# Token lists of a mixture of experts: scattered through DRAM slots instead of built by one-hot matmuls

## The chip, the cores and the metric

One core of a Trainium2 chip runs the kernel. The metric is the device time in microseconds (us). Engines: TensorE (PE, with its weight loads as PEld), VectorE (DVE), ScalarE (ACT), GpSimd (POOL) and SyncE (SP). SP, ACT and POOL also start transfers (DMAs). Each engine works through its own instructions in the order in which the program wrote them.

## The reference

```python
x = attention in chunks of 64 over q, k, v (8 batches, 8 heads, 576 positions, 64 wide)   # -> x[4608, 512]
logits = x @ w_gate + log1p(exp(x @ w_noise)) * noise          # [4608, 8]
top2   = the two experts with the largest logits;  top2_w = softmax over those two
for e in range(8):
    for k in range(2):
        mask = top2[:, k] == e
        h = np.maximum(x[mask] @ w1[e], 0.0)                   # w1[e] is 512 x 1024
        out[mask] += top2_w[mask, k, None] * (h @ w2[e])       # w2[e] is 1024 x 512
```

Each token goes to two experts. For each expert the kernel needs a list: which tokens are its own, and with which weight.

## The kernel before

**Attention.** `attend(it)` runs a software pipeline over 36 tiles of 128 tokens: scores of tile `it` (line 407), maximum and subtraction on DVE (L411, L416), the transposes of tile `it-2` (L423), the values of tile `it-3` (L434), their division (L439 to L446, tile `xs`), the store of the finished tile to the DRAM tensor `xbuf`, and its transposes for the gate (L454). Six leftover steps of the pipeline (`tail`) are put between the matmuls of the first expert block.

**Routing.** Tiles are routed in five groups, g0 to g4, of 8, 8, 4, 8 and 8 tiles. `route(g)` is a generator; `step_route(n)` advances it by n steps, and the calls of it in `attend` and in the hooks between matmuls set where in each engine's order its work stands. It finds the two experts of each token, counts with small matmuls how many earlier tokens went to the same expert, and so gets in `lii` the slot of each of the two entries of a token: slot = 8 * (row in the expert's list) + expert. `vals` holds the entry: token number and weight.

**Lists.** With 10 row blocks of 128 and 8 experts a list is the tile `acc` [128, 2, 80]. For each token tile two one-hot factors are built: `gohp` (128 tokens by 128 rows within a block; POOL and ACT, L595 to L597) and `grhs` (128 tokens by 2 x 80 values: `geq` on DVE, L599, times the entry, L603, on POOL or, in g4, DVE). `place` multiplies them on PE (L587, two f32 matmuls of 160 columns a tile, summed in PSUM over a group); `acc` adds the groups up (L619, L621). `finish_lists` (L202 to L206, five DVE operations) turns a part of `acc` into row numbers `lid` and weights `lwt`.

**Experts.** The work is 24 blocks (`BL`), three for each expert. The first expert's blocks are `EARLY`: block 0 needs g0 and g1 only, block 1 needs g0 to g3, block 2 all groups. `gather(i)` fetches a block's rows from `xbuf` on POOL (L235), `x_tile` turns them (PE transposes L283, `xh` and `xl` by L290 and L291), `layer1` and `layer2` multiply (L300, three matmuls for each product, on high and low parts), with `hh` on ACT (L318), `hl` on DVE (L319). `layer1(0)` has two PSUM banks in turn, so its part f+2 waits for the `hl` of part f. The other experts are handled in the order of their load, so `acc` is put in that order (L634, L636) and `pieces` makes indices of quarter rows; from block 3 on the rows are fetched in quarters (L255). `store` adds a block's result to `out` in DRAM (L267, an indirect DMA that adds). `out` is first filled with zeros by 37 DMAs on SP (L665).

The program as built lets an indirect DMA start only when the eighth one before it has landed.

Of the kernel before, what the change touches and what calls it, by code (L numbers as in the profile page):

```python
# [8 lines left out]
FT = mybir.dt.float32  # L9
FR = mybir.dt.float32r  # L10
BF = mybir.dt.bfloat16
I32 = mybir.dt.int32
# [48 lines left out]
def kernel(ctx, tc, qT, kT, vh, wgn, noise, w1, w2, out, caps=CAPS):  # L61
# [18 lines left out]
    row = consts.tile([P, P], FT, name="row")  # L80
    nc.gpsimd.iota(row, pattern=[[1, P]], base=0, channel_multiplier=0, allow_small_or_imprecise_dtypes=True)
    e_row = row[:, 0:NE]

    row_p = consts.tile([P, P], FT, name="row_p")
    nc.gpsimd.iota(row_p, pattern=[[NE, P]], base=0, channel_multiplier=0, allow_small_or_imprecise_dtypes=True)
    row_je = consts.tile([P, NLIST, NE], FT, name="row_je")
    nc.gpsimd.iota(row_je, pattern=[[NE * P, NLIST], [1, NE]], base=0, channel_multiplier=0, allow_small_or_imprecise_dtypes=True)
# [73 lines left out]
    xg = ctx.enter_context(tc.tile_pool(name="xg", bufs=5))  # L161


    NL = NJ * NE
    acc = consts.tile([P, 2, NL], FT, name="acc")
    lid = consts.tile([P, NJ, NE], I32, name="lid")
    lwt = consts.tile([P, NJ, NE], FT, name="lwt")
    lfl = consts.tile([P, NJ, NE], FT, name="lfl")
# [7 lines left out]
        nc.vector.memset(part[q * 32:q * 32 + 32], float(q))  # L176
    xpieces = xbuf.rearrange("r (q c) -> (r q) c", c=P)
    opieces = out.rearrange("r (q c) -> (r q) c", c=P)
    HF = {}
    XG, XH, HT, BX, BH, OB = {}, {}, {}, {}, {}, {}  # L180
    rot = {"xg": 0, "tr": 0, "l1": 0, "l2": 0}
# [18 lines left out]
    def finish_lists(to_row, to_weight, rows, a):  # L200

        nc.vector.tensor_copy(to_weight, a[:, 1])  # L202
        nc.vector.tensor_scalar(rows, a[:, 0], col[:, 1:2], None, op0=OP.add)
        nc.vector.scalar_tensor_tensor(rows, a[:, 1], 0.0, rows, op0=OP.is_gt, op1=OP.mult)
        nc.vector.tensor_scalar(rows, rows, col[:, 0:1], None, op0=OP.add)
        nc.vector.tensor_copy(to_row, rows)  # L206
# [211 lines left out]
    def soft_exp(t):  # L418
        nc.scalar.activation(PR[t], PR[t], AF.Exp, scale=0.125)
# [56 lines left out]
    def route(g):  # L476
# [95 lines left out]
            V.tensor_reduce(lii[:, :, ts], ohr, AX.X, OP.add)  # L572
# [4 lines left out]
        V.tensor_scalar(pj[:, 0], lii[:, :, ts], NE * (P - 1), None, op0=OP.bitwise_and)  # L577
        V.tensor_tensor(pj[:, 1], lii[:, :, ts], pj[:, 0], OP.subtract)
        V.tensor_copy(pf, pj)  # L579
        yield  # L580

        lp = PS[:, 7, 0:2 * NL]
        built = []

        def place(r, ohp, rhs):
            for k in range(2):
                nc.tensor.matmul(lp, ohp[:, k], rhs[:, k].rearrange("p c n -> p (c n)"),  # L587
                                 start=(r == 0 and k == 0), stop=(r == G - 1 and k == 1))

        B = nc.gpsimd if g < LAST else V  # L590
        n2 = [P, 2, NL]
        for r in range(G):
            t = t0 + r
            ohp = gate.tile([P, 2, P], FT, name="gohp", bufs=3)
            nc.gpsimd.tensor_scalar(ohp[:, 0], row_p, pf[:, 0, 0, r:r + 1], None, op0=OP.is_equal)  # L595
            nc.scalar.activation(ohp[:, 1], row_p, AF.Abs, scale=-1.0, bias=pf[:, 0, 1, r:r + 1])
            nc.scalar.activation(ohp[:, 1], ohp[:, 1], AF.Relu, scale=-1.0, bias=1.0)  # L597
            eq = gate.tile(n2, FT, name="geq", bufs=3)
            V.tensor_tensor(eq, row_je.rearrange("p j e -> p (j e)")[:, None, :].to_broadcast(n2),  # L599
                            pf[:, 1, :, r:r + 1].to_broadcast(n2), OP.is_equal)  # L600
            yield
            rhs = gate.tile([P, 2, 2, NL], FT, name="grhs", bufs=3)
            B.tensor_tensor(rhs, eq[:, :, None, :].to_broadcast([P, 2, 2, NL]),  # L603
                            vals[:, :, t, :, None].to_broadcast([P, 2, 2, NL]), OP.mult)
            yield
            yield
            built.append((r, ohp, rhs))
            if len(built) > 2:
                yield
                place(*built.pop(0))  # L610
            yield
        while built:
            for _ in range(3):
                yield
            place(*built.pop(0))
        yield
        av = acc.rearrange("p c n -> p (c n)")
        if g == 0:
            V.tensor_copy(av, lp)  # L619
        else:  # L620
            V.tensor_add(av, av, lp)  # L621
        a4 = acc.rearrange("p c (j e) -> p c j e", e=NE)
        for i in EARLY:
            if g == EARLY[i]:
                js = slice(blocks[0][i][0][0], blocks[0][i][-1][0] + 1)
                finish_lists(lid0[i], lwt0[i], lfl[:, js, 0], a4[:, :, js, 0])
                gather(i)
        if g == LAST:
            for c in range(2):
                for js in (slice(0, NJ // 2), slice(NJ // 2, NJ)):  # L630
                    n = [P, js.stop - js.start, NE, NE]
                    by = gate.tile([P, 2, 2, NL], FT, name="grhs", bufs=3).rearrange("p a b n -> p (a b n)")
                    by = by[:, 0:n[1] * NE * NE].rearrange("p (j r e) -> p j r e", r=NE, e=NE)
                    V.tensor_tensor(by, a4[:, c, js][:, :, None, :].to_broadcast(n),  # L634
                                    perm[:, None].to_broadcast(n), OP.mult)
                    V.tensor_reduce(accp[:, c, js], by, AX.X, OP.add)  # L636
                    yield
            finish_lists(lid, lwt, lfl, accp)

    routing = []  # L640

# [8 lines left out]

    ordered = []

    def finish_route(until=lambda: not routing):
# [72 lines left out]
    def hook_tail(f, d):  # L726
        if d == 0 and f % 2 == 0 and f >= 2:
            if f == 2:
                zero_out(10)
            zero_out(9)  # L730
        if d % 2 and tail and (f, d) != (0, 3):
            attend(tail.pop(0))
        else:
            step_route(2)

    for i in range(NBL + 1):
        e, b = BL[i] if i < NBL else (NE, 0)
# [37 lines left out]
        if 1 < i < NBL and i == 3:  # L775
            layer2(i - 1, hook2_f)
        if i < NBL:
            layer1(i, hook1, hook_tail if i == 0 else lambda f, d: step_route(1))
        split1 = halves if (i < NBL and b == nb - 1 and e + 1 < NE) else []
        split1_e = e + 1  # L780

# [157 lines left out]
```

## Time and profile before

| | |
|---|---|
| Median of 3 runs | 1025.91 us (1025.23 to 1027.11) |
| The profiled execution | 1026.64 us, span 1024.7 us |
| Its mean granted TensorE clock | 0.977 |
| Busy | PE 970.7, PEld 864.3, DVE 461.7, ACT 300.8, POOL 475.5 us |

The attention takes roughly the first 150 us of the span, the first expert's three blocks with the end of the routing the next 130, and the other experts the rest. Rows of a timeline give the start, the length, the engine, the line and operation with its tiles, how many instructions were merged, and in brackets how long the engine was idle before and what ended that. Rows of the chain of work that ended last give start, length, engine and line. Rows of stretches give, for each engine, busy time and instruction count, then the granted clock, the share of the DMA engines' time and GB/s.

### The profile page before, as it was taken

Reading aid. Unit: us, or ns where it says so; the run is one execution under the profiler, and the core shown is the slowest. Engines: PE = TensorE matmul, PEld = TensorE weight load, DVE = VectorE, ACT = ScalarE, POOL = GpSimd, SP = SyncE. Lnnn points to the kernel's source line nnn. Section 1 sums busy time; section 2 is a strip of 40 time slices with the busy share of each in tenths; the row PEclk is TensorE's granted clock in tenths of the full one; section 3 lists DMA queues with packets and bytes.
Section 4 is the critical chain, followed back from the end, with each engine's and each line's share of the span. In section 5 each row is a group of like instructions: output and inputs, shape, how many; then the busy total and the mean of one; then the engine's idle time right before and its main releaser. Section 6 shows DMA issues by size and latency. Waiting matters only on the chain.

```text
span 1024.7 us, 18328 instructions
## 1 busy us (share of the span) xinstructions
PE 970.7 (95%) x7353; PEld 864.3 (84%) x7353; DVE 461.7 (45%) x1037; ACT 300.8 (29%) x649; POOL 475.5 (46%) x613
## 2 busy tenths in 40 slices
PE   6888978999799999999999999999999999999995
PEld 4677757898679899889988998899989998899884
DVE  5587765644334444344424533453245334434311
ACT  3466644331223232123212321231123222323100
POOL 1043523425767467436743775378336734611111
PEclk9889989999899999999999999999999999999998
DMA  9997891232251335233533353335333434412213
GB/s 365 397 326 275 302 380 43 46 95 75 60 141 44 88 89 137 49 82 90 135 49 83 98 128 55 83 101 126 55 104 97 98 66 105 124 27 31 32 21 42
DMA packets 51943, 121.51 MB, mean 119 GB/s; under 512 B 8288, under 2 KB 9184, under 8 KB 51856
## 3 DMA queue, kind: packets, MB, share of 16 engines
q0 software_dynamic: 20160, 38.69, 20.6%
q1 hardware_dynamic: 26512, 72.20, 19.3%
q10 hardware_dynamic: 5184, 9.44, 2.4%
q8 instruction: 58, 0.95, 0.4%
q14 instruction: 29, 0.24, 0.1%
HBM read 81.56 MB, written 38.73 MB: 117 GB/s over the span
## 4 chain that ended last, share of the span: by engine, by line
PE 87%; DVE 5%; DMA 3%; issue 2%; ACT 1%; SPq 1%; POOL 0%; DVEq 0%; ACTq 0%
PE PS L300 79%; DMA out<-zero 2%; PE PS L587 1%; PE PS L434 1%; PE PS L407 1%; SPq L665 1%; PE PS L423 1%; PE PS L329 1%; DVE xs L446 1%; DVE pr L416 1%; DVE mx L411 1%; PE PS L454 1%; PE PS L472 1%; DMA st<-in_w 1%; PE PS L461 0%
## 5 line engine op out<-in xcount | busy, mean ns | idle before, releaser
L255 POOL DMA_INDIRECT xg<-xbuf,piece x257 | 259.4, 1009 | 77.2 <-issue 62.3
L300 PE MATMUL PS<-xh,w1h 128*128 128x384 f32 (+2 forms) x768 | 264.0, 344 | 4.3 <-issue 1.9
L300 PE MATMUL PS<-xh,w1l 128*128 128x384 f32 (+2 forms) x768 | 261.9, 341 | 2.5 <-issue 2.5
L300 PE MATMUL PS<-xl,w1h 128*128 128x384 f32 (+2 forms) x768 | 262.1, 341 | 1.6 <-issue 1.3
L300 PE MATMUL PS<-w2h,hh 128*128 128x512 f32 x584 | 228.7, 392 | 0.0
L300 PE MATMUL PS<-w2h,hl 128*128 128x512 f32 x584 | 227.8, 390 | 0.1
L300 PE MATMUL PS<-w2l,hh 128*128 128x512 f32 x584 | 227.7, 390 | 0.0
L267 POOL DMA_INDIRECT out<-o,lid x73 | 116.8, 1600 | 227.8 <-DVE o L338 208.8
L319 DVE SCALAR_TENSOR_TENSOR hl<-PS,hh 128x384 fp32r<-128x384 f32 (+1 forms) x192 | 107.1, 559 | 246.1 <-ACT hh L318 185.2
L318 ACT ACTIVATE hh<-PS 128x384 fp32r<-128x384 f32 (+1 forms) x192 | 94.0, 491 | 374.7 <-PE PS L300 316.7
L300 PEld LDWEIGHTS PS<-xh,w1h 128*128 128x128 f32 x768 | 145.2, 189 | 9.0 <-issue 3.8
L300 PEld LDWEIGHTS PS<-xl,w1h 128*128 128x128 f32 x768 | 145.1, 189 | 5.4 <-issue 3.0
L300 PEld LDWEIGHTS PS<-xh,w1l 128*128 128x128 f32 x768 | 145.2, 189 | 3.4 <-issue 2.4
L338 DVE TENSOR_SCALAR o<-PS,lwt 128x512 f32<-128x512 f32 x73 | 54.5, 749 | 190.3 <-PE PS L300 153.5
L300 PEld LDWEIGHTS PS<-w2h,hl 128*128 128x128 f32 x584 | 109.2, 187 | 23.9 <-issue 0.5
L300 PEld LDWEIGHTS PS<-w2h,hh 128*128 128x128 f32 x584 | 109.2, 187 | 23.1 <-issue 0.8
L300 PEld LDWEIGHTS PS<-w2l,hh 128*128 128x128 f32 x584 | 109.2, 187 | 22.8 <-issue 0.4
L290 ACT ACTIVATE xh<-y 128x512 fp32r<-128x512 f32 x67 | 41.2, 614 | 101.2 <-DVE y L287 72.8
L291 DVE TENSOR_TENSOR xl<-y,xh 128x512 fp32r<-128x512 f32 x67 | 44.9, 671 | 48.0 <-ACT xh L290 33.5
L595 POOL TENSOR_SCALAR gohp<-row_p,gpf 128x128 f32<-128x128 f32 x36 | 24.2, 674 | 71.8 <-DVE gpf L579 54.2
L287 DVE STREAM_TRANSPOSE y<-xg 128x512 f32<-128x512 f32 x67 | 45.6, 680 | 0.0
L136 DVE TENSOR_TENSOR w2l<-st,w2h 128x512 fp32r<-128x512 f32 x64 | 44.5, 695 | 0.0
(138 smaller groups left out, 788.6 us busy)
## 6 DMA issues: line engine op xcount, KB each, us to landing
st<-in_w SPq DMA_DIRECT2D x64, 512.0 KB
out<-zero SPq DMA_DIRECT2D x37, 256.0 KB
vb<-in_vh SPq DMA_DIRECT2D x18, 520.0 KB
qp<-in_qT SPq DMA_DIRECT2D x18, 512.0 KB
kb<-in_kT SPq DMA_DIRECT2D x18, 512.0 KB
xbuf<-xs ACTq DMA_DIRECT2D x36, 256.0 KB
xg<-xbuf,piece POOLq DMA_INDIRECT x257
out<-o,lid POOLq DMA_INDIRECT x73
```

Of the source, the lines that this page charges most:

```text
L136: (eng or nc.vector).tensor_sub(lo[:, s], st[:, s], hi[:, s].bitcast(FT))
L255: nc.gpsimd.indirect_dma_start(out=XG[e, j][:, t * P:(t + 1) * P], out_offset=None, in_=xpieces, in_offset=bass.IndirectOffsetOnAxis(ap=pi ...
L267: s = nc.gpsimd.indirect_dma_start(out=to, out_offset=bass.IndirectOffsetOnAxis(ap=rows, axis=0), in_=o, in_offset=None, compute_op=OP.add)
L287: nc.vector.transpose(y[:, 0:4 * r], x[:, 0:4 * r])
L290: nc.scalar.activation(oh, src, AF.Copy)
L291: nc.vector.tensor_sub(ol, src, oh.bitcast(FT))
L300: nc.tensor.matmul(p, a, b, start=first and n == 0, stop=last and n == 2)
L318: nc.scalar.activation(hh[:, 0:m], p, AF.Relu)
L319: nc.vector.scalar_tensor_tensor(hl[:, 0:m], p, 0.0, hh[:, 0:m].bitcast(FT), op0=OP.max, op1=OP.subtract)
L329: nc.tensor.matmul(p[32 * q:32 * q + 32, 0:P], HF[0][:, f, 32 * t:32 * t + 32], w[:, q * P:(q + 1) * P], start=(f == 0), stop=(f == NF - 1))
L338: nc.vector.tensor_scalar(o[0:r], p[0:r], weights_of(i, j)[0:r], None, op0=OP.mult)
L595: nc.gpsimd.tensor_scalar(ohp[:, 0], row_p, pf[:, 0, 0, r:r + 1], None, op0=OP.is_equal)
```

## The change

The one-hot factors, their matmuls and the sums in `acc` are gone. The list is now the first 10 * 128 * 8 slots of the DRAM tensor `lists`, 8 bytes each (`slots`), filled with zeros by one DMA on SP at the start. `place_one(t, k)` scatters the 128 entries of token tile t and choice k straight from `vals` to the slots in `lii`, with an indirect DMA on POOL: 72 of them, each behind a one-element memset. When the groups that a block needs are scattered, SP loads the part of the list back (`acc0` for blocks 0 and 1, the whole `acc` for the rest), and `finish_lists` works on that. These steps stand in a queue `moves`, first in, first out, with five empty places between a load and its use; `step_moves` takes 3 of them in each step of the attention, 1 in each hook of `layer1(0)`, and 1 in every second hook after that.

```diff
+    slots = lists[0:NJ * P * NE, :].bitcast(FT)
+    by_slot = slots.rearrange("(j p e) c -> p j e c", p=P, e=NE)
...
+    nc.sync.dma_start(slots.rearrange("(p a) c -> p (a c)", p=P), zero[:, 0:2 * NJ * NE])
...
-        pj = gate.tile([P, 2, 2, G], I32, name="gpj")
-        pf = gate.tile([P, 2, 2, G], FT, name="gpf")
...
-            for k in range(2):
-                nc.tensor.matmul(lp, ohp[:, k], rhs[:, k].rearrange("p c n -> p (c n)"),
-                                 start=(r == 0 and k == 0), stop=(r == G - 1 and k == 1))
...
-            nc.gpsimd.tensor_scalar(ohp[:, 0], row_p, pf[:, 0, 0, r:r + 1], None, op0=OP.is_equal)
-            nc.scalar.activation(ohp[:, 1], row_p, AF.Abs, scale=-1.0, bias=pf[:, 0, 1, r:r + 1])
-            nc.scalar.activation(ohp[:, 1], ohp[:, 1], AF.Relu, scale=-1.0, bias=1.0)
...
-            V.tensor_tensor(eq, row_je.rearrange("p j e -> p (j e)")[:, None, :].to_broadcast(n2),
-                            pf[:, 1, :, r:r + 1].to_broadcast(n2), OP.is_equal)
...
-            B.tensor_tensor(rhs, eq[:, :, None, :].to_broadcast([P, 2, 2, NL]),
-                            vals[:, :, t, :, None].to_broadcast([P, 2, 2, NL]), OP.mult)
...
-            V.tensor_add(av, av, lp)
...
+        moves.extend(lambda t=t, k=k: place_one(t, k) for t in range(t0, t0 + G) for k in range(2))
         for i in EARLY:
+            if g == EARLY[i] and g < LAST:
                 js = slice(blocks[0][i][0][0], blocks[0][i][-1][0] + 1)
-                finish_lists(lid0[i], lwt0[i], lfl[:, js, 0], a4[:, :, js, 0])
-                gather(i)
+                moves.append(lambda i=i, js=js: read.append(nc.sync.dma_start(acc0[i], by_slot[:, js, 0, :])))
+                moves.extend([None] * 5)
+                moves.append(lambda i=i, js=js: (finish_lists(lid0[i], lwt0[i], lfl[:, js, 0], acc0[i].rearrange("p j c -> p c j")),
+                                                 gather(i)))
...
+            moves.append(lambda: nc.sync.dma_start(acc.rearrange("p j e c -> p j (e c)"),
+                                                   by_slot.rearrange("p j e c -> p j (e c)")))
+            moves.extend([None] * 5)
...
+    def place_one(t, k):
+        nc.gpsimd.memset(spacer, 0.0)
+        d = nc.gpsimd.indirect_dma_start(
+            out=lists, out_offset=bass.IndirectOffsetOnAxis(ap=lii[:, k, t:t + 1], axis=0),
+            in_=vals[:, k, t, :].bitcast(I32), in_offset=None)
...
+        step_moves(3 if it <= NT else 0)
...
+        step_moves(1)
...
+            step_moves(1 - f % 2)
```

**SP's order at the end of the attention.** Before, the last loads of q, k and v are followed by the loads of the first expert's second weights and the zeros of `out` (`order` is the expert order, needed later):

```order
L368 DMA qp<-in_qT 128x1024
L372 DMA kb<-in_kT 128x1024
L376 DMA vb<-in_vh 128x1040
L124 DMA st<-in_w 128x2x512 x4
L665 DMA out<-zero 128x512 x37
L791 TENSOR_LOAD order
```

With the change (`acc_111` and `acc_112` are the list parts of blocks 0 and 1):

```order
L370 DMA kb<-in_kT 128x1024
L374 DMA vb<-in_vh 128x1040
L119 DMA st<-in_w 128x2x512
L578 DMA acc_111<-lists 128x3x2
L119 DMA st<-in_w 128x2x512 x3
L650 DMA out<-zero 128x512 x28
L578 DMA acc_112<-lists 128x3x2
L650 DMA out<-zero 128x512 x9
L779 TENSOR_LOAD order
```

Three weight loads and all zeros now stand behind the load of the first list part, and nine zeros behind the second.

**POOL's order at the gather of block 0.** Before, one-hot work of groups 1 and 2 is on either side of the three gathers:

```order
L595 TENSOR_SCALAR gohp<-row_p,gpf 128x128
L603 TENSOR_TENSOR grhs<-geq,vals 128x320
L235 DMA xg<-xbuf,lid_118 128x512 x3
L595 TENSOR_SCALAR gohp<-row_p,gpf 128x128
L603 TENSOR_TENSOR grhs<-geq,vals 128x320
```

With the change:

```order
L607 MEMSET spacer 1x1
L608 DMA lists<-vals,lii 44032x2
L233 DMA xg<-xbuf,lid_116 128x512 x3
L607 MEMSET spacer 1x1
L608 DMA lists<-vals,lii 44032x2
```

All 32 scatters of g0 and g1 stand ahead of the gathers, and the 24 of g2 and g3 between these and the gathers of block 1.

**DVE's order in `layer1(0)`.** Before, `hl` of part 4 (`hl_2633`), a weight split, one-hot work, `hl` of part 5, and the list of block 1 only after part 6:

```order
L319 SCALAR_TENSOR_TENSOR hl_2633<-PS,hh_2632 128x384
L136 TENSOR_TENSOR w2l_3010<-st,w2h_3009 128x512
L599 TENSOR_TENSOR geq<-row_je,gpf 128x160 x2
L319 SCALAR_TENSOR_TENSOR hl_2635<-PS,hh_2634 128x384
L136 TENSOR_TENSOR w2l_3010<-st,w2h_3009 128x512
L319 SCALAR_TENSOR_TENSOR hl_2637<-PS,hh_2636 128x384
L136 TENSOR_TENSOR w2l_3077<-st,w2h_3076 128x512
L621 TENSOR_TENSOR acc<-acc,PS 128x160
L202 COPY lwt_122<-acc 128x3
```

With the change (`hl_2519` is part 4, `hl_2521` part 5):

```order
L317 SCALAR_TENSOR_TENSOR hl_2519<-PS,hh_2518 128x384
L131 TENSOR_TENSOR w2l_2864<-st,w2h_2863 128x512
L510 MAX gm<-gsp 128x8 x6
L514 MAX_INDEX gmi<-gm,gsp 128x8 x8
L519 TENSOR_TENSOR goh<-row,gmi 128x64
L200 COPY lwt_120<-acc_112 128x3
L201 TENSOR_SCALAR lfl<-acc_112,col 128x3
L202 SCALAR_TENSOR_TENSOR lfl<-acc_112,lfl 128x3
L203 TENSOR_SCALAR lfl<-lfl,col 128x3
L204 CAST lid_117<-lfl 128x3
L317 SCALAR_TENSOR_TENSOR hl_2521<-PS,hh_2520 128x384
```

The list of block 1 moved ahead of `hl` of part 5, and routing of g4 stands where the one-hot work stood. In the same way the list of block 0 now stands in the attention behind the subtraction of tile 33 (before: tile 30), and that of block 2 behind `hl` of part 4 of `layer1(1)`.

More of the change, by code (lines that the diff above doesn't have):

```diff
@@ L79 @@
     spacer = consts.tile([1, 1], FT, name="spacer")
-    row = consts.tile([P, P], FT, name="row")
-    nc.gpsimd.iota(row, pattern=[[1, P]], base=0, channel_multiplier=0, allow_small_or_imprecise_dtypes=True)
+    row = consts.tile([P, NE], FT, name="row")
+    nc.gpsimd.iota(row, pattern=[[1, NE]], base=0, channel_multiplier=0, allow_small_or_imprecise_dtypes=True)
     e_row = row[:, 0:NE]
[L84 to L87, printed above, removed]
     vals = consts.tile([P, 2, NT, 2], FT, name="vals")
@@ L161 @@
     xg = ctx.enter_context(tc.tile_pool(name="xg", bufs=5))
-    NL = NJ * NE
-    acc = consts.tile([P, 2, NL], FT, name="acc")
+    acc = consts.tile([P, NJ, NE, 2], FT, name="acc")
+    acc0 = {b: consts.tile([P, len(blocks[0][b]), 2], FT, name=f"acc0{b}") for b in EARLY if EARLY[b] < 4}
     lid = consts.tile([P, NJ, NE], I32, name="lid")
@@ L178 @@
     opieces = out.rearrange("r (q c) -> (r q) c", c=P)
+    slots = lists[0:NJ * P * NE, :].bitcast(FT)
+    by_slot = slots.rearrange("(j p e) c -> p j e c", p=P, e=NE)
+    placed, read = [], []
     HF = {}
@@ L590, in route @@
[L590 to L595, printed above, removed]
-            nc.scalar.activation(ohp[:, 1], row_p, AF.Abs, scale=-1.0, bias=pf[:, 0, 1, r:r + 1])
-            nc.scalar.activation(ohp[:, 1], ohp[:, 1], AF.Relu, scale=-1.0, bias=1.0)
-            eq = gate.tile(n2, FT, name="geq", bufs=3)
-            V.tensor_tensor(eq, row_je.rearrange("p j e -> p (j e)")[:, None, :].to_broadcast(n2),
-                            pf[:, 1, :, r:r + 1].to_broadcast(n2), OP.is_equal)
-            yield
-            rhs = gate.tile([P, 2, 2, NL], FT, name="grhs", bufs=3)
-            B.tensor_tensor(rhs, eq[:, :, None, :].to_broadcast([P, 2, 2, NL]),
-                            vals[:, :, t, :, None].to_broadcast([P, 2, 2, NL]), OP.mult)
[L605 to L620, printed above, removed]
-            V.tensor_add(av, av, lp)
[L622 to L625, printed above, removed]
-                finish_lists(lid0[i], lwt0[i], lfl[:, js, 0], a4[:, :, js, 0])
-                gather(i)
@@ L628, in route @@
[L628 to L638, printed above, removed]
+        moves.extend(lambda t=t, k=k: place_one(t, k) for t in range(t0, t0 + G) for k in range(2))
@@ new lines, in route, with reorder @@
+        for i in EARLY:
+            if g == EARLY[i] and g < LAST:
+                js = slice(blocks[0][i][0][0], blocks[0][i][-1][0] + 1)
+                moves.append(lambda i=i, js=js: read.append(nc.sync.dma_start(acc0[i], by_slot[:, js, 0, :])))
+                moves.extend([None] * 5)
+                moves.append(lambda i=i, js=js: (finish_lists(lid0[i], lwt0[i], lfl[:, js, 0], acc0[i].rearrange("p j c -> p c j")),
+                                                 gather(i)))
+        if g == LAST:
+            a4 = acc.rearrange("p j e c -> p c j e")
+            def reorder(c, js):
+                n = [P, js.stop - js.start, NE, NE]
+                by = gate.tile([P, NJ * NE * NE // 2], FT, name="gby", bufs=2)
+                by = by[:, 0:n[1] * NE * NE].rearrange("p (j r e) -> p j r e", r=NE, e=NE)
+                V.tensor_tensor(by, a4[:, c, js][:, :, None, :].to_broadcast(n),
+                                perm[:, None].to_broadcast(n), OP.mult)
+                V.tensor_reduce(accp[:, c, js], by, AX.X, OP.add)
+            moves.append(lambda: nc.sync.dma_start(acc.rearrange("p j e c -> p j (e c)"),
+                                                   by_slot.rearrange("p j e c -> p j (e c)")))
+            moves.extend([None] * 5)
+            for i in EARLY:
+                if EARLY[i] == LAST:
+                    js = slice(blocks[0][i][0][0], blocks[0][i][-1][0] + 1)
+                    moves.append(lambda i=i, js=js: (finish_lists(lid0[i], lwt0[i], lfl[:, js, 0], a4[:, :, js, 0]), gather(i)))
+            moves.extend(lambda c=c, js=js: reorder(c, js) for c in range(2) for js in (slice(0, NJ // 2), slice(NJ // 2, NJ)))
+            moves.append(lambda: finish_lists(lid, lwt, lfl, accp))
@@ new lines, in route @@
+        yield
+    moves = []
+    def place_one(t, k):
[3 more added lines that the diff above has]
+            in_=vals[:, k, t, :].bitcast(I32), in_offset=None)
+        for o in placed:
+            tc.declare_no_dep(d.ins, o.ins, reason="each token and expert has a slot of its own")
+        for o in read:
+            tc.declare_no_dep(d.ins, o.ins, reason="slots that were read are not written afterwards")
+        placed.append(d)
@@ L640, with step_moves @@
+    def step_moves(n):
+        for _ in range(n):
+            if moves:
+                move = moves.pop(0)
+                if move:
+                    move()
     routing = []
@@ L651, with finish_route @@
     ordered = []
-    def finish_route(until=lambda: not routing):
+    def finish_route(until=lambda: not routing and not moves):
         while not until():
             step_route(1)
+            step_moves(1)
     halves = [(c, h) for c in range(4) for h in range(2)]
@@ L734, in hook_tail @@
             step_route(2)
+        step_moves(1)
     for i in range(NBL + 1):
@@ L777 @@
         if i < NBL:
-            layer1(i, hook1, hook_tail if i == 0 else lambda f, d: step_route(1))
+            layer1(i, hook1, hook_tail if i == 0 else lambda f, d: (step_route(1), step_moves(1 - d % 2)))
         split1 = halves if (i < NBL and b == nb - 1 and e + 1 < NE) else []
```

6 lines of the change are left out of this document (removed).

## The prediction

> **What bounds the kernel now.** I read the page's busy times first, then stretches of the span, then the chain of work that ended last, then each engine's timeline around the lists. The first row is the page's, the others are stretches (length; busy time and count of PE, PEld, DVE, ACT, POOL; granted clock; DMA share; GB/s).
>
> ```profile
> PE 970.7 (95%) x7353; PEld 864.3 (84%) x7353; DVE 461.7 (45%) x1037; ACT 300.8 (29%) x649; POOL 475.5 (46%) x613
> 100.00:125.00 25.00, 23.59 (x493) 20.15 (x491) 17.53 (x53) 15.91 (x40) 10.71 (x16) 0.93 0.84 291
> 175.00:200.00 25.00, 25.00 (x146) 22.65 (x145) 13.57 (x59) 9.98 (x26) 10.48 (x14) 1.00 0.19 43
> 260.60:269.20 8.60, 2.83 (x7) 1.31 (x7) 1.94 (x3) 1.17 (x2) 6.72 (x10) 0.74 0.55 85
> ```
>
> PE bounds the whole span. In the expert stage it has no gap, so work taken from it there is time gained in full. In the attention it is nearly full, in a ring of PE and DVE steps, so removal there gains at most its PE time. The last row is an exception, a hole of 8.6 us in which PE did 2.8 us of work.
>
> **What is removed.** The one-hot matmuls: the tile's answer, then pieces of the chain (start, length).
>
> ```profile
> L587 PE MATMUL PS<-grhs,gohp x144: 297/299/403, 73.9 to 228.1; 128*128 128x160 f32 x144
> 81.57 1.28 PE PS L587 x8
> 207.87 0.54 PE PS L587 x4
> 208.42 2.61 PE PS L300 x15
> 211.03 0.54 PE PS L587 x4
> ```
>
> 144 records are 36 tiles of 4. Between expert matmuls one tile takes 0.54 us of the chain; 16 tiles (g3 in `layer1(0)`, g4 in `layer1(1)`) lie there: 16 x 0.54 = 8.6 us, all gained. The other 20 lie in the attention. There two tiles take 1.28 us, so 20 x 0.64 = 12.8 us is the upper bound. For the lower one I use the pace of the scores, one row a tile of tokens:
>
> ```profile
> 43.37 0.69 PE L407 MATMUL PS<-kb,qp 64*64 64x64 f32 x32
> 56.76 1.13 PE L407 MATMUL PS<-kb,qp 64*64 64x64 f32 x32
> 73.14 0.86 PE L407 MATMUL PS<-kb,qp 64*64 64x64 f32 x32
> 89.34 0.69 PE L407 MATMUL PS<-kb,qp 64*64 64x64 f32 x32
> 108.96 0.69 PE L407 MATMUL PS<-kb,qp 64*64 64x64 f32 x32
> 126.31 0.69 PE L407 MATMUL PS<-kb,qp 64*64 64x64 f32 x32 [1.15 <-DVE mx L411]
> 142.12 0.69 PE L407 MATMUL PS<-kb,qp 64*64 64x64 f32 x32 [1.06 <-DVE pr L416]
> 149.09 1.09 PE L283 MATMUL PS<-ident,xg 128*128 128x128 f32 x8
> ```
>
> Four steps without lists (43.37 to 56.76) take 13.4 us, 3.35 each. With g0 four take 16.2 (2.8 more), with g1 17.35 (3.95 more), and the step with g2 6.97 (3.6 more): 10.4 us. I take 11.5, the middle. The one-hot work on POOL, ACT and DVE leaves with it; it stood beside PE and is in these differences. Gross gain: 11.5 + 8.6 = 20.1 us.
>
> **What is added.** 72 scatters on POOL, 72 memsets, three list loads on SP, and one 80 KB zero fill on SP early in the attention, which by the zeros quoted below (37 x 256 KB in 36.4 us) is 0.3 us of transfer and is put at nothing. No scatter of this kind is in the trace. The nearest rows:
>
> ```profile
> L267 POOL DMA_INDIRECT out<-o,lid x73: 1487/1616/1643, 195.2 to 1013.6; - x73
> L235 POOL DMA_INDIRECT xg<-xbuf,lid x10: 911/974/1205, 125.2 to 234.5; - x10
> 292.17 0.96 POOL L255 DMA_INDIRECT xg<-xbuf,piece  x1 [0.30 <-issue]
> 293.12 0.09 POOL L266 MEMSET spacer<- 1x1 f32 x1
> 293.43 1.62 POOL L267 DMA_INDIRECT out<-o,lid  x1 [0.21 <-issue]
> ```
>
> A gather of 128 rows is 0.97 us, a store that adds is 1.62. A scatter goes to DRAM like the store, but it neither adds nor moves 2 KB rows. I take 0.96; with memset and gap (293.43 less 293.12) that is one every 1.27 us. Both ends stay for the range: 1.27 to 1.93. POOL's busy time falls little; its 72 x 1.27 = 91 us do not matter in themselves. What matters is that a list is now ready only after its last scatter has landed and SP has loaded it back, and that DVE waits for it in order. The places:
>
> ```profile
> 68.18 1.27 POOL L136 TENSOR_TENSOR w1l<-st,w1h 128x512 fp32r<-128x512 f32 x1 [1.22 <-ACT w1h L135]
> 71.18 0.66 POOL L595 TENSOR_SCALAR gohp<-row_p,gpf 128x128 f32<-128x128 f32 x1 [1.73 <-DVE gpf L579]
> 103.55 0.29 DVE L572 TENSOR_REDUCE lii<-gohr 128x16 int32<-128x128 f32 x1
> 125.17 1.21 POOL L235 DMA_INDIRECT xg<-xbuf,lid  x1 [4.37 <-DVE lid L206]
> 127.94 0.96 POOL L235 DMA_INDIRECT xg<-xbuf,lid  x1 [0.30 <-issue]
> 188.03 1.05 POOL L235 DMA_INDIRECT xg<-xbuf,lid  x1 [4.96 <-DVE lid L206]
> 192.08 0.60 PE L283 MATMUL PS<-ident,xg 128*128 128x128 f32 x4
> ```
>
> Landing: the gather that ended at 189.1 was read at 192.1 without a wait, so it takes at most 3.0 us after its generation. I use 3 for the last scatter and another 3 for SP's load (small pieces, no row; between 1 and 8).
>
> The Trainium skill ("DMA: Bandwidth & Descriptors", section "Anatomy of one DMA — SWDGE (gpsimd) path") gives a fixed cost of about 2.0 us for a DMA, most of it the receipt of the last write. The trace's bound agrees with it; with 2 for 3 twice in each chain the waits below would shrink by about 2 us, to 1010, an estimate from that page.
>
> *Block 0's list.* g0's slots are there at 70.4; 16 x 1.27 and two more weight splits (1.3 each) keep POOL until 93.4. g1's slots come at 103.9 less the 3.1 that g0 has gained, 101: 16 x 1.27 to 121.3, loaded by 127.3. DVE needs it behind the subtraction of tile 33:
>
> ```profile
> 133.88 1.14 PE L407 MATMUL PS<-kb,qp 64*64 64x64 f32 x32
> 135.81 0.69 DVE L416 TENSOR_TENSOR pr<-PS,mx 128x512 f32<-128x512 f32 x1
> 112.06 2.74 SPq L124 DMA_DIRECT2D st<-in_w  x4
> 114.85 36.38 SPq L665 DMA_DIRECT2D out<-zero  x37
> ```
>
> 136.5 less 7.5 (g0 and g1) is 129.0: 1.7 us to spare. I put 0.5 for it. With 0.9 for the five operations the gathers start at 130.4, end at 134.2, and land at 138 with the zeros around them (SP stands still until 124, so these now start 10 us later); PE wants them at 149.09 less 11.5 = 137.6. Another 1.0. `x_tile(0)` starts at 139.1. The three weight loads held up on SP are wanted after 145, and have 20 us.
>
> *Block 1's list.* g2's 8 scatters end at 144.4. g3's slots come about 6.3 us after `x_tile(0)`, 145.4: 16 more to 165.7, loaded by 171.7. The rows of this stage:
>
> ```profile
> 153.23 0.45 PE L300 MATMUL PS<-xh,w1h 128*128 128x384 f32 x1 [1.41 <-DVE xl L291]
> 179.16 0.56 DVE L319 SCALAR_TENSOR_TENSOR hl<-PS,hh 128x384 fp32r<-128x384 f32 x1 [1.66 <-ACT hh L318]
> 187.28 0.39 PE L300 MATMUL PS<-w2h,hh 128*128 128x512 f32 x1
> 206.53 0.44 PE L300 MATMUL PS<-xh,w1h 128*128 128x384 f32 x1 [0.96 <-ACT xh L290]
> 228.14 0.51 PE L300 MATMUL PS<-w2h,hh 128*128 128x512 f32 x1
> ```
>
> The first matmul stands 4.1 us behind `x_tile(0)`, `hl` of part 4 25.9 us later, less four tiles (2.2): 166.9, and with the work behind it DVE asks at 168.4. It waits 3.3 us; behind it stand `hl` of part 5 and the gate's one-hot tile that PE's count of g4 needs. PE has parts 5 and 6 to do, 2 x 12 x 0.174 = 4.2 us, before part 7 needs that `hl`. With 0.9 for the list and 0.6 for `hl` PE stands about 2.5 us.
>
> *Block 2's list.* `layer2(0)` starts at 139.1 + 38.2 - 4.3 + 2.5 = 175.5, `layer1(1)` 19.25 later, 194.8. POOL has the gathers of block 1 until 176.4, then 16 scatters among three stores: 20.3 + 3 x 1.93 after 177.5, 203.6; loaded by 210.6 (1,280 pieces). DVE asks at about 206 and waits 4.6; PE has parts 5 to 7 (6.3 us) and five parts of `layer2(1)` ahead. Cost 1.0. The first store stands on POOL between scatters and waits for the last nine zeros, which SP issues only after 168; they take 9 x 0.98, and the store is wanted at 181, so they are just in time.
>
> **Sum.** 20.1 - 0.5 - 1.0 - 2.5 - 1.0 = 15.1 us. The profiled execution took 1026.64 (0.73 above the median): 1011.5, and 0.7 less against the median. I keep 1012. About 0.2% (2 us) is what a measurement of this kernel can tell from no change.
>
> **The rivals.**
> 1. *A scatter costs what a store costs, and the lists come late: slower.* Place: DVE's first list operation. At 1.93 each, g0 ends at 103.9, g1 at 134.8, loaded at 140.8: DVE, and with it the attention, stands 12 us. Then 24 scatters from 145.5 end at 192, loaded at 198 against 181: PE stands 11.5, and the gathers add 1.5. 16 scatters and three stores from 205 are loaded at 248 against 230: PE stands about 12. Together 37 against 20.1: 1043.5. Between 5 us of waits at 1.27 and 37 at 1.93 it breaks even near 1.58, a scatter of 1.27 us. For it: the destination in DRAM. Against it: the gather has as many indices, and the store's add is missing.
> 2. *Cheap scatters, but slow landing or slow loads of small pieces,* 11 us instead of 6 each: the three waits grow by about 4.5, 4 and 3: 1023. For it: the DMA share is 0.84 at 100 to 125. Against it: SP, blocked by the load itself, sends nothing large meanwhile.
> 3. *No list is late:* 1026.6 - 20.1 = 1006.5. The hole at 260.6, which the profile puts down to no other engine, may go too when PE's instructions shift: up to 8.6 - 2.8 = 5.8 more, 1001; or another may open, 6 more.
> 4. *DVE holds up POOL's generation.* The gather at 125.17 took 1.21 us beside DVE, the last of its three 0.96. If every scatter in the attention took 1.21, g1 would be loaded at 135 and the first list cost 6 more: about 1020. If DVE stretched generation fivefold, to 4.8 us, 32 scatters would end near 234, and block 0 would start about 100 us late: 1110. The Trainium skill ("SBUF — State Buffer", section "SBUF: two separate sides") warns of this: a GpSimd DMA of about 620 ns takes about 3100 ns beside a copy on VectorE that uses both port pairs. By that rule it would be the fivefold case; the trace's gathers, at most 1.21 beside DVE, speak against it.
>
> **How the numbers follow.** Forecast, 1007 to 1019: 0.52. Rival 3, below 1007: 0.11. Rival 2 and the mild form of rival 4, 1019 to 1028, centre 1022: 0.17. Rival 1, 1028 to 1050: 0.18. Rival 4's fivefold case: 0.02. Faster (below 1024) is 0.52 + 0.11 + 0.12 = 0.75; the same (1024 to 1028) 0.05; slower 0.20. The range 1003 to 1034 leaves out about 0.04 below and 0.15 above. The forecast's own range is 1007 to 1019.
>
> **What would show it.** Scatters of 0.9 to 1.1 us on POOL; no L587 rows; `layer1(1)` with 17.3 us of PE instead of 21.6; DVE idle for 1 to 5 us ahead of the first `lwt` copy of each block, ended by a DMA; `x_tile(0)` near 139. Scatters of 1.3 us or more, DVE waiting over 8 us at a list, or PE empty in `layer1(0)`, would make the prediction wrong.

## The result and the profile after

The changed kernel takes 1084.24 us (median; 1081.15 to 1088.92), the kernel before, beside it, 1025.57 (1024.66 to 1027.11): ratio 1.0574, 95% interval 1.0531 to 1.0617. The change is 58.7 us slower, where the prediction was 1012 us. The profiled execution took 1088.92 us, its span is 1087.1 (before 1024.7). The page's first line, and the answer for the tile `lists`:

```profile
PE 976.6 (90%) x7209; PEld 863.8 (79%) x7209; DVE 443.9 (41%) x973; ACT 279.6 (26%) x577; POOL 509.5 (47%) x691
```

```profile
L608 POOL DMA_INDIRECT lists<-vals,lii x72: 958/968/1154, 71.5 to 281.2; - x72
...
  DVE lwt L200: 8.3, 1
```

The removal and the price of a scatter came out as predicted: no one-hot matmul is left (144 records fewer), a scatter takes 0.968 us where 0.96 was taken, and the worst stretches it to 1.154. Only one list was waited for, for 8.3 us. All that is no reason for 59 us. The loss is all in the part that holds the scatters: `x_tile(0)` starts here,

```profile
193.88 1.97 PE L281 MATMUL PS<-ident,xg 128*128 128x128 f32 x8
```

44.8 us later than before (149.09), and by the first matmul of block 3 the lag is 60.0 us (361.7 against 301.7); the span ends 62.4 later. Stretches of that part, columns as in the prediction's rows:

```profile
75.00:100.00 25.00, 16.98 (x175) 11.34 (x176) 6.17 (x12) 5.97 (x11) 16.42 (x30) 0.55 0.39 128
121.00:144.00 23.00, 7.99 (x90) 6.09 (x94) 2.85 (x10) 1.83 (x4) 16.74 (x31) 0.52 0.28 84
201.00:224.00 23.00, 8.40 (x73) 6.23 (x71) 0.00 (x0) 1.90 (x4) 16.77 (x31) 0.65 0.07 17
252.00:282.00 30.00, 29.07 (x153) 26.08 (x152) 7.12 (x14) 4.26 (x8) 21.69 (x37) 1.00 0.40 89
```

Where POOL sends 16 scatters in a row (31 POOL records: 16 scatters, 15 memsets), everything else stands: from 121 to 144 us PE runs 90 matmuls where the stretch 100 to 125 of the kernel before had 493 in 25 us; from 201 to 224 DVE runs nothing at all (it waits for ACT's `hh`, below). The DMA engines are mostly idle too (shares 0.28 and 0.07), so it is not bandwidth that is short. PE's granted clock is low in these rows (0.52 and 0.65), but that can't be the whole cause, since ACT stands as well. Only in the last row, between wide matmuls and with stores among the scatters, does PE go on. PE's timeline inside the second row, and POOL's first and last scatter of it:

```profile
126.69 0.34 PE L406 MATMUL PS<-kb,qp 64*64 64x64 f32 x1 [0.97 <-issue]
128.13 0.37 PE L406 MATMUL PS<-kb,qp 64*64 64x64 f32 x2 [1.10 <-issue]
129.55 0.38 PE L406 MATMUL PS<-kb,qp 64*64 64x64 f32 x2 [1.05 <-issue]
130.98 0.38 PE L406 MATMUL PS<-kb,qp 64*64 64x64 f32 x2 [1.04 <-issue]
133.10 0.26 PE L406 MATMUL PS<-kb,qp 64*64 64x64 f32 x1 [1.75 <-issue]
...
140.19 0.27 PE L433 MATMUL PS<-vb,pts 64*64 64x65 f32 x1 [1.75 <-issue]
141.61 0.26 PE L433 MATMUL PS<-vb,pts 64*64 64x65 f32 x1 [1.16 <-issue]
143.71 0.59 PE L433 MATMUL PS<-vb,pts 64*64 64x65 f32 x10 [1.84 <-issue]
```

```profile
120.95 0.97 POOL L608 DMA_INDIRECT lists<-vals,lii  x1 [22.97 <-DVE vals L572]
...
140.04 0.97 POOL L608 DMA_INDIRECT lists<-vals,lii  x1 [0.22 <-issue]
```

One or two matmuls start, then nothing for a multiple of 0.7 us (126.69, 128.13, 129.55: 1.43 apart), and "issue" says that PE waits for nothing that the profile shows. 2.7 us after the last scatter is generated (141.0) all runs again. ACT shows the same with its input long there: PE's part for `hh` ended by 207.7, and ACT, idle from 205.7, takes it at 223.79, again 2.7 us after the row's end.

```profile
205.11 0.59 ACT L462 ACTIVATE ls<-PS 128x512 f32<-128x512 f32 x1
223.79 0.49 ACT L316 ACTIVATE hh<-PS 128x384 fp32r<-128x384 f32 x1 [18.09 <-remote]
```

With this in view the kernel before reads differently. The hole at 260.60 to 269.20, quoted in the prediction, lies at the end of a row of 14 gathers and two stores (243.5 to 264.6), and its seven matmuls start 0.7, 1.4 or 2.1 us apart. And later, beside POOL's gathers, DVE and ACT have idle time that nothing explains (waits: total us, times, longest):

```profile
DVE hl L319 <- issue: 45.2, 25, 3.8
ACT hh L318 <- remote: 32.0, 9, 10.1
```

It costs next to nothing there: from the first matmul of block 3 to the end this profile takes 723.0 us, and a later one of the same kernel, without such idle time, 722.5. PE is the bound there, and with its wide matmuls it starts few instructions in a microsecond.

### The profile page after: what moved, and what is told of

The parts are those of the page before. It is cut to its first block, busy times and chain, and to the rows that moved or that the text cites. A ratio compares the mean times of both kernels' runs of the same rounds, so it can differ in the third digit from the quotient of the medians.

```text
span 1087.1 us, 17953 instructions
## 1 busy us (share of the span) xinstructions
PE 976.6 (90%) x7209; PEld 863.8 (79%) x7209; DVE 443.9 (41%) x973; ACT 279.6 (26%) x577; POOL 509.5 (47%) x691
## 4 chain that ended last, share of the span: by engine, by line
PE 80%; DVE 7%; another core or an unknown queue 4%; issue 4%; DMA 1%; POOL 1%; ACT 1%; SPq 0%; DVEq 0%; POOLq 0%; ACTq 0%
PE PS L298 71%; PE PS L433 2%; PE PS L406 2%; PE PS L422 1%; PE PS L453 1%; DVE mx L410 1%; DVE pr L415 1%; DVE xs L445 1%; PE PS L327 1%; POOL lists L608 1%; PE PS L460 1%; PE PS L471 1%; DMA lists<-vals,lii 0%; PE PS L281 0%
## 5 line engine op out<-in xcount | busy, mean ns | idle before, releaser
L253 POOL DMA_INDIRECT xg<-xbuf,piece x257 | 261.0, 1016 | 80.8 <-issue 64.9
L608 POOL DMA_INDIRECT lists<-vals,lii x72 | 70.1, 973 | 60.9 <-DVE vals L572 44.2
L433 PE MATMUL PS<-vb,pts 64*64 64x65 f32 x1152 | 38.4, 251 | 46.4 <-issue 18.7
L433 PEld LDWEIGHTS PS<-vb,pts 64*64 64x64 f32 x1152 | 30.0, 158 | 53.6 <-issue 22.4
```

What stands on the lines that cost most here:

```text
L253: nc.gpsimd.indirect_dma_start(out=XG[e, j][:, t * P:(t + 1) * P], out_offset=None, in_=xpieces, in_offset=bass.IndirectOffsetOnAxis(ap=pi ...
L433: nc.tensor.matmul(PS[s, 3 + h, hp * 65:hp * 65 + 65], PT[t][r, hp, s], v[r, t % 2, c, hp, :], start=True, stop=True)
L608: d = nc.gpsimd.indirect_dma_start(out=lists, out_offset=bass.IndirectOffsetOnAxis(ap=lii[:, k, t:t + 1], axis=0), in_=vals[:, k, t, :].bi ...
```

## The experiments

**1. Without scatters, and with scatters that nothing reads.** Theory A: scatters in unbroken rows hold up the other engines. B: the lists are late. C: something else that moved. The first kernel has no scatters, and a fixed list in the slots:

```diff
-    nc.sync.dma_start(slots.rearrange("(p a) c -> p (a c)", p=P), zero[:, 0:2 * NJ * NE])
+    nc.sync.dma_start(by_slot.rearrange("p j e c -> p j (e c)"), fixed.rearrange("p j e c -> p j (e c)"))
...
         nc.gpsimd.memset(spacer, 0.0)
-        d = nc.gpsimd.indirect_dma_start(
```

> The changed kernel without its 72 scatters (the memsets and the three list loads stay; the slots hold a fixed list of valid rows, written once at the start, so every block gathers and stores as many rows as before, but not the right ones). Theory A, the generation of scatters in unbroken rows on POOL holds up the other engines: everything lost comes back, 1000 to 1012 us, PE idle for no reason that the profile shows falls from 42 us to about 10. Theory B, the lists come late and DVE waits for them: also about 1006. Theory C, the loss lies in what else moved (zeros late on SP, list loads, DVE's order): above 1050.

The second sends the 72 scatters to a tensor that nothing reads (`out=dump` for `out=lists`), the third has gathers in their place, in the fourth POOL works on SBUF in place of every second one.

> As the kernel without scatters, fixed list and all, but with the 72 scatters at their old places, to a DRAM tensor that nothing reads, so no list load waits for them. Theory A: the loss stays, 1065 to 1090 us, with holes of PE at 75 to 100, 121 to 143 and 173 to 185 us. Theory B: it goes, 1000 to 1012.

> The same, but each scatter is a gather of the same 128 entries of 8 bytes from DRAM to an SBUF tile that nothing reads. Theory A (any indirect DMA, it is POOL's generation that counts): 1065 to 1090 us. Rival A2 (it is the small writes to DRAM that clog the DMA engines or the memory): 1000 to 1015.

> As the kernel with unread scatters, but the scatter of every second entry is replaced by a POOL operation of 128x256 elements, about 1 us: 36 scatters, one per 2.5 us, over the same time. If each scatter costs the same, half the loss stays: 1035 to 1050 us. If an unbroken row of them is needed (theory A as the holes that grow within a row suggest it): 1005 to 1020.

Measured, against 1016.21 us for the kernel before on the same chip: without scatters 1002.18 (ratio 0.9858, 0.9809 to 0.9908), unread 1015.45 (0.9987, 0.9965 to 1.0008), gathers 1009.25 (0.991, 0.9858 to 0.9961), half and spaced 1008.39 (0.9919, 0.9891 to 0.9948). The first is what A and B both expect; against C it says little on this chip, but the same kernel falls below the kernel before on a chip that shows the loss, too (group 4), so C falls. The second looks like the end of A: 72 scatters in rows up to 20 us long, and no hole. But the kernel before is 9 us faster here too, and DVE and ACT show no unexplained idle time in any of the four. So theory D: the stops belong to the chip, or to something that holds on it at the time.

**2. Both kernels again, on one chip.**

> The changed kernel as it is, once more, beside the kernel before on the same chip. Theory A (unbroken rows of scatters stop the engines because a list load or a reader waits on them, which the kernel with unread scatters did not have): 1065 to 1090 us, holes in PE as in the first profile. Theory D (the stop belongs to the chip on which the first two profiles were taken: there DVE has 88 us and ACT 51 us of idle time that nothing explains in the kernel before too, and the four kernels above show none at all): 1008 to 1025 us on a chip whose profile shows no such idle time, 1075 or more on one that does.

> The kernel before, once more, for its profile on this chip. Theory D: where the changed kernel does not stop, this one shows no hole near 260 us, and no idle time of DVE and ACT that nothing explains, and takes 1014 to 1020 us; where it does stop, the hole of 8.6 us is there and it takes 1025. Theory A: the hole is there in both cases.

The changed kernel took 1020.99 us, the kernel before 1016.23 (1.0071, 1.0039 to 1.0104); the second copy of the kernel before 1016.3 (1.0, 0.9979 to 1.0022). D holds. The stretch that was the hole, in this profile of the kernel before:

```profile
260.60:269.20 8.60, 8.60 (x44) 7.95 (x43) 4.24 (x7) 2.94 (x6) 7.42 (x10) 1.00 0.61 94
```

PE full with 44 matmuls where it had 7, beside as many POOL operations (10). The change is slower here as well, by 4.8 us, and for other reasons (below).

**3. The unread scatters on a chip that stops.** This chip's kernel before took 1023.10 us.

> The kernel with 72 unread scatters once more, on whatever chip this is. Where the kernel before takes about 1016 us and has no unexplained idle time: 1012 to 1019. Where it takes about 1025 and has its hole near 260 us, theory D in its strong form (POOL's rows of indirect DMAs stop the other engines there, whether or not anything waits for the data) says 1060 or more; if the stops need a wait for the lists, 1025 to 1035.

1078.07 us (1.0537, 1.0494 to 1.058): the same kernel that cost nothing on the other chip. Nothing waits for these scatters, so B falls for the large loss. The stretch 120 to 140 us of it, and of the same kernel without stops:

```profile
120.00:140.00 20.00, 7.62 (x69) 5.77 (x71) 2.93 (x15) 2.47 (x5) 11.86 (x23) 0.50 0.29 96
```

```profile
120.00:140.00 20.00, 15.11 (x365) 12.20 (x367) 12.43 (x30) 9.69 (x21) 8.59 (x16) 0.93 1.05 361
```

69 matmuls against 365. The lists loaded by POOL instead of SP (`nc.gpsimd.dma_start` for `nc.sync.dma_start` at the three loads), on the same chip:

> The changed kernel with its three list loads issued by POOL instead of SP. In the second profile of the changed kernel SP stood from 110.6 to 123.1 us at the first list load, the weight loads and zeros behind it came 14 us late, and ACT stood 8.5 us at a store of xbuf until one of these weight loads had landed. Theory E (the loss is SP's wait, passed on to ACT by the landings that its stores wait for): SP issues the weights and zeros at 109 to 113 us again, ACT's wait of 8.5 us goes, x_tile(0) comes 4 to 9 us earlier, 1012 to 1017 us on a chip where the changed kernel takes 1021. Theory B (DVE waits for a late list, whoever loads it): 1019 or more. On a chip of the first kind, with stops, 1070 or more by theory D.

1085.37 us (1.0595, 1.0557 to 1.0632), as the changed kernel itself: who loads the lists does not matter where the engines stop (the unread scatters say the same: they cost 55.0 us with no list late). Theory E, which was about the chips without stops, was not tried there by this run.

**4. What in a row stops them.** The kernels of the first group again, and one more, where a scatter of every second entry is left out without anything in its place. The kernel before took 1027.51 us on this chip.

> The kernel without scatters (fixed list) on whatever chip this is. Where the kernel before takes about 1016 us: 1000 to 1005, as the first time. Where it takes about 1024 (stops): theory D says that all of the loss goes with the scatters, 1006 to 1016, and no hole in PE before 240 us.

> 72 gathers of 8-byte entries from DRAM, to a tile that nothing reads, in place of the scatters. With stops: any indirect DMA in a row does it, 1060 to 1085 us; or only writes to DRAM do, 1010 to 1025. Without stops: 1005 to 1012, as the first time.

> 36 unread scatters, each followed by a POOL operation of about 1 us on SBUF. With stops: if the unbroken row is what counts, nearly all of the loss goes, 1010 to 1025 us; if each scatter costs its share, 1040 to 1050. Without stops: 1005 to 1010, as the first time.

> 36 unread scatters back to back, so rows half as long (10 us in place of 20). With stops: if a row costs from its first DMA on, half of the loss stays, 1038 to 1048 us; if the engines stand only from some 4 us into a row on, as the first DVE waits of a row do, less than half, 1020 to 1038. Without stops: 1005 to 1010.

Without scatters 1016.88 us (0.9898, 0.9835 to 0.9961); gathers 1079.27 (1.0505, 1.0467 to 1.0544); half and spaced 1019.50 (0.9928, 0.9895 to 0.9961); half in rows 1035.40 (1.0067, 1.0027 to 1.0107). The stretch 120 to 140 us with gathers, then with spaced scatters:

```profile
120.00:140.00 20.00, 6.35 (x48) 4.50 (x47) 3.10 (x18) 1.84 (x4) 12.03 (x23) 0.50 0.29 93
```

```profile
120.00:140.00 20.00, 16.52 (x376) 13.55 (x376) 12.03 (x30) 8.79 (x19) 6.41 (x10) 0.84 1.05 378
```

Gathers do it as scatters do, so it is neither the write to DRAM nor its 8 bytes: it is that POOL generates indirect DMAs. And it is the row: 36 of them, one per 2.18 us with 0.87 us of POOL's own work between, cost 2.6 us over none; 36 in rows of 8 cost 18.5; 72 in rows of 16 cost 62 (gathers here), more than three times as much for twice the number. Whether the gap in time counts, or that POOL does other work in it, was not separated.

```profile
160.34 1.03 POOL L617 DMA_INDIRECT dump<-vals,lii  x1 [0.19 <-issue]
161.38 0.09 POOL L613 MEMSET spacer<- 1x1 f32 x1
161.44 0.87 POOL L615 TENSOR_SCALAR pad<-zero 128x256 f32<-128x256 f32 x1
162.24 0.09 POOL L613 MEMSET spacer<- 1x1 f32 x1
162.52 1.02 POOL L617 DMA_INDIRECT dump<-vals,lii  x1 [0.18 <-issue]
```

**5. Looking for a faster version.** One-hot lists where PE has time (g0 to g2), scatters for the last groups, the slots added to `acc`:

```diff
+        if g >= HOT:
+            moves.extend(lambda t=t, k=k: place_one(t, k) for t in range(t0, t0 + G) for k in range(2))
...
+                        nc.vector.tensor_add(part0[i], a4[:, :, js, 0], acc0[i].rearrange("p j c -> p c j")),
```

> One-hot lists for g0 to g2, inside the attention, and scatters for g3 and g4 only (32 of them); the loaded slots are added to acc. Theory F (at the end of the attention a chain of transfers sets the time, so PE time taken away there is worth little, 4 us in place of the 11.5 predicted, while the 8.6 us between expert matmuls are worth their full time): the attention stays at 145 us, layer1(0) becomes 3 to 4 us shorter, layer1(1) 0 to 3, so 1009 to 1013 us where the kernel before takes 1016. If PE time in the attention counts too (the prediction's step), the loss of 20 tiles' gain puts it at 1016 or more. With stops: 1040 to 1060.

> Scatters for g4 only (16). Theory F: only the 8 one-hot tiles between the matmuls of layer1(1) go, 3.2 us as the kernel without scatters showed, against a list of block 2 that comes later: 1012 to 1016 us where the kernel before takes 1016. With stops: within 10 us of the kernel before, since a row of 16 scatters with stores between them left PE at 29.1 of 30 us there.

Both on a chip with stops: 1028.20 us (1.0048, 1.0028 to 1.0069) and 1027.11 (1.0044, 1.0031 to 1.0058) against 1023.10; the first lost less than expected, the second lost 4.0 us, within what was expected. A row of scatters can stop PE among wide matmuls too: in the first of them PE, with its 384-column matmuls, stands 3.65 us before 180.07, inside the row of 16 scatters from 163.2 to 184.0. Then pauses after every fourth DMA: one POOL operation in the row of gathers of the kernel before and in the kernel with unread scatters (the code below), two shorter ones in the mixed kernel.

```diff
+        if len(placed) % 4 == 0:
+            nc.gpsimd.tensor_scalar(pad, zero[:, 0:PADN], 1.0, None, op0=OP.mult)
```

> The kernel before, with one POOL operation of 0.9 us after every fourth of the 14 quarter gathers that stand in one row at 243 to 261 us. With stops: if a row of 4 is short enough, the hole of 8.6 us goes and the time falls by 5 to 8 us; if a pause of 0.9 us does not end the stop, it stays. Without stops there is no hole: within 2 us of the kernel before.

> One-hot lists for g0 to g2 and scatters for g3 and g4, as in the earlier run of that kind (1028.2 us with stops, where the kernel before took 1023.1), now with a pause of about 1 us on POOL after every fourth scatter and every fourth gather of the first row of quarter gathers. With stops: the holes at 176 to 180 us and near 270 us go, 8 to 14 us faster than that run, so 4 to 9 us faster than the kernel before. Without stops: 1008 to 1013 where the kernel before takes 1016. If list lateness rather than the stops made that run slow: no better than it.

> 72 unread scatters with a POOL operation of 0.9 us after every fourth. With stops: if rows of 4 are short enough, within 10 us of the kernel without scatters (10 us below the kernel before), so from 10 us below to the time of the kernel before; if the pause does not help, 40 us or more above the kernel before. Without stops: 1010 to 1018.

> The kernel before with a POOL operation of 0.9 us after every fourth of the 14 quarter gathers in one row, once more. With stops (the kernel before at 1022 us or more): if a pause after four ends the stop, the hole of 8.6 us near 260 us goes and the time falls by 5 to 8 us; if it does not, no change. Without stops: no change, as the first time.

All four fell on chips without stops: 1014.90 us (0.9993, 0.9974 to 1.0012), 1016.40 (1.0009, 0.9992 to 1.0026), 1015.97 (1.0004, 0.9988 to 1.002), 1015.47 (0.9997, 0.9977 to 1.0018). So whether a pause after four is enough stays open, and no version here beats the kernel before. The mixed kernel missed its 1008 to 1013, and the waits of its profile say why: what PE saved went into the wait for block 1's list and its gathers.

```profile
PE PS L297 <- DMA xg<-xbuf,lid: 10.2, 1, 10.2
DVE part L599 <- DMA acc<-lists: 8.9, 1, 8.9
```

**All runs side by side,** in us against the kernel before on the same chip:

| kernel | chips without stops | chips with stops |
|---|---|---|
| the change | +4.8 | +58.7 |
| no scatters | -14.0 | -10.6 |
| 72 unread scatters | -0.8 | +55.0 |
| 72 unread gathers | -7.0 | +51.8 |
| 36 unread, spaced | -7.8 | -8.0 |
| 36 unread, in rows of 8 | | +7.9 |
| lists loaded by POOL | | +62.3 |
| scatters for g3 and g4, for g4 | | +5.1, +4.0 |
| scatters for g3 and g4, paused | +1.7 | |
| unread, rows of 4 | +1.3 | |
| the kernel before, gathers paused | +0.2, -0.1 | |

By the intervals above, each of these differences is known to some 2 to 7 us only; those under 2 us are no difference. The 4.8 us of the change, for one, have an interval of 4.0 to 10.6.

## Why the prediction was wrong

**The step that failed: "POOL's busy time falls little; its 72 x 1.27 = 91 us do not matter in themselves."** They do. On the chip of the forecast, rows of POOL's indirect DMAs stop PE, DVE and ACT. The scatters alone, with nobody waiting, cost 65.6 us on chips that stop (55.0 + 10.6, from two chips) and 13.3 on one that does not (14.0 - 0.8). What they write and who waits is the small part: the change less the unread scatters is 3.7 us with stops, 5.5 without. (Nor did POOL's busy time fall: the 72 scatters and memsets weigh more than the one-hot work that left, 509.5 against 475.5 us.)

The sign of it was quoted: the hole at 260.60, "which the profile puts down to no other engine". The prediction gave it 5.8 us in either direction and asked neither what POOL did there nor why DVE had 45 us of waits for "issue". A row of 14 gathers stood right ahead of it, and the change makes four rows as long and puts three of them among small matmuls, where PE needs some 40 instructions a microsecond instead of 10.

**The rivals.** None is this mechanism. Rival 4 had the two engines right and the direction wrong: POOL's generation did not stretch (the median scatter or unread gather takes 0.95 to 1.03 us in every run, stops or none, and the longest 1.45), the others stood. The Trainium skill ("SBUF — State Buffer", section "Who interferes with whom") says that of the engines only VectorE and GpSimd share SBUF ports, and that PE and ACT never wait on anyone there. In these traces PE and ACT do stand inside POOL's rows (18.09 us at `hh`), so, by that rule, the stop is not the port lock that rival 4 was about. Rival 1 (a scatter costs a store's time) is out by the 0.968 us. Rival 2 is out too: on the chip without stops the last scatter was generated by 218.45, the load of block 2's list was issued at 222.47 after its landing, and DVE had it at 225.92: 7.5 us for both, where the sum had 7 for this list and rival 2 had 11.

**What stops them** is not shown. The form of it (a few instructions, then none for a multiple of 0.7 us, on PE, with nothing to wait for) looks like that of an engine that isn't handed instructions. The Trainium skill ("Runtime: NRT & Kernel Launch", section "Instruction fetch mechanics") says that each engine's instructions are fetched ahead in blocks of 16 KiB over a DMA queue of its own, and that this is mostly hidden. The page agrees on the blocks (57 packets in 0.93 MB), but the DMA records speak against the landing of such blocks as the cause: none begins from 194.6 to 228.3 us, while ACT stands from 207.5 to 223.8 and then goes on, and from 121 to 144, where PE runs 90 matmuls, only two half blocks do.

The records of semaphore updates in the traces point elsewhere. In every profile without stops they are nearly complete and come at once: in the kernel before, 528 for the 525 instructions that raise PE's semaphore, 264 for 262 of POOL's. In every profile with stops many are late or missing (490 and 179 in the first profile of the kernel before). In the row from 201 us the last two instructions of PE that raise the semaphore for which ACT waits start at 208.3 and 211.7, the next updates of it are recorded at 223.73 to 223.97, and ACT goes on at 223.79: by these records it stood for a signal that came 12 us late or more. PE's own steps have no semaphore between them, so this is not all of it. No run separates these causes, nor a chip from what holds on it at the time, and each execution timed here was traced (each has a granted clock on record): whether the engines stop without a trace is not shown.

**The sum, on a chip without stops.** There the prediction can be held against its own terms, and was still wrong: 15.1 us gained was forecast, 4.8 lost was measured. Gross gain: 20.1 predicted, 14.0 measured (the kernel without scatters, two executions: the interval is 9 to 19, and the two profiles compared here are 10.7 us apart). Starts of `x_tile(0)` and of the next expert stages, kernel before:

```profile
145.05 1.09 PE L283 MATMUL PS<-ident,xg 128*128 128x128 f32 x8
...
205.01 0.44 PE L300 MATMUL PS<-xh,w1h 128*128 128x384 f32 x1 [0.96 <-ACT xh L290]
```

and without scatters:

```profile
141.05 1.95 PE L284 MATMUL PS<-ident,xg 128*128 128x128 f32 x8
...
197.46 0.45 PE L301 MATMUL PS<-xh,w1h 128*128 128x384 f32 x1
```

Of the 8.6 us between expert matmuls, 3.6 came in this stage (59.96 to 56.41) and 3.2 in the next (to the first matmul of block 2: 249.4 and 238.66). That step was right in kind and good to 2 us. The attention gave 4.0 in place of 11.5: this term of the sum was sized too large. The pace of the scores was the wrong measure, because, by the chain, transfers set the attention's end (no run took them away). The chain of the kernel without scatters, from 115 us on:

```profile
115.96 8.56 DMA out<-zero
...
125.42 5.45 DMA out<-zero
...
136.52 6.28 DMA out<-zero
142.81 0.33 ACTq L454
```

Zeros of `out` land one behind the other, and the last store of `xbuf` on ACT's queue waits for one of them. The same chain stands in the kernel before (a zero from 140.50 to 145.66, then ACT's store). The prediction quoted a sign of it, the DMA share of 0.84, and used it only for landing times. A part of the gain seems to have gone to the granted clock: without scatters it was 0.79 from 125 to 150 us, against 1.00 in the kernel before, and the same eight transposes of `x_tile(0)` take 1.95 us in place of 1.09 (rows above).

Costs: 5.0 predicted, 18.8 measured: 13.3 for the scatters themselves and 5.5 for the waits, a rough split, with the intervals above. The waits were near: DVE stood once, 7.36 us at block 2's list (4.6 predicted), never at block 0's or 1's. But the wait at block 0's list went another way than the sum had it, through SP and ACT. SP's order, then ACT's:

```profile
109.40 1.16 SPq L119 DMA_DIRECT2D st<-in_w  x1
123.08 0.37 SPq L578 DMA_DIRECT2D acc<-lists  x1
123.55 1.47 SPq L119 DMA_DIRECT2D st<-in_w  x3
125.07 27.04 SPq L650 DMA_DIRECT2D out<-zero  x28
```

```profile
127.94 0.33 ACTq L451 DMA_DIRECT2D xbuf<-xs  x1
128.31 0.60 ACT L454 ACTIVATE xt<-PS 128x512 f32<-128x512 f32 x1 [8.48 <-DMA st<-in_w]
```

"The three weight loads held up on SP ... have 20 us" was wrong: ACT's store of `xbuf` waits until one of them has landed (in this program the two use one semaphore in turn), so SP's 12.5 us at the list became 8.5 us of ACT. `x_tile(0)` came at 152.65, 11.6 later than without scatters; 7.8 of these are there with unread scatters too (148.89), so at most 3.8 come this way, read from the profiles and not tested by a run. The 13.3 us of scatters that nobody waits for are about 0.18 each (36 of them cost 6.2, but 72 gathers in their place only 7.1); by which engine they reach PE is open. The granted clock is one candidate: over the span it was 0.965 to 0.977 with unread scatters and 0.980 without any.

## What to carry to other kernels

Look for idle time that "nothing" ends, on engines that cost nothing by it, and at what runs beside it: it can grow when the work there changes. Do not line up POOL's indirect DMAs in long rows beside work of many small instructions; put other POOL work between them (one operation each was enough for 36 of them here). Before you count time taken from an engine, follow the chain to the end of its stage: where transfers set it, the gain is theirs, and a load that waits on a queue holds up those who wait for the transfers behind it.

## What the runs showed of the hardware

Chips differ. The chip of the first profiles and two numbered ones (the first may be one of the two) stop inside POOL's rows, four others do not; the kernel before takes 1023 to 1028 us on the former and 1015 to 1016 on the latter, and the change costs 58.7 or 4.8 us. The stop is not in POOL, whose scatters take 0.968 and 0.967 us on the two. PE suffers most among small instructions: it is busy for 7.99 of 23 us beside 16 scatters among 64-column matmuls, and for 29.07 of 30 beside 16 scatters and stores among wide ones. Wide matmuls are no safeguard, though: the hole of 8.6 us and the 3.65 us above lie among them. Where the engines stop, the trace also lacks records of semaphore updates, a sign that can be looked for in one profile.
